# Gated linear attention and a two-expert router in one kernel: router weights through SyncE, routing regrouped into thirteen steps, first gathers of x issued later in their stage

## The chip, the cores and the metric

The kernel runs on one core of a Trainium2 chip. The metric is the device time of one execution in microseconds. Three runs of the kernel before took 773.51, 774.62 and 775.79 us; their median is 774.62 us. A separate execution was recorded by the hardware profiler; all timelines below are from it.

Engines are named as the profile names them: PE is TensorE (PEld its weight loads), DVE is VectorE, ACT is ScalarE, POOL is GpSimd, SP is SyncE, which only issues DMAs. A name with a q (ACTq, SPq) is an engine's queue, here the issue of DMAs.

## What is computed

The first block is a recurrence over 768 positions for 4 batches and 8 heads of 48 dimensions. Its output, as 3072 rows x of 384 numbers, feeds a router that picks two of eight experts for each row; each expert is a two-layer network.

```python
for t in range(S):
    state = alpha[:, :, t, :, None] * state + einsum('bhd,bhe->bhde', k[:, :, t], v[:, :, t])
    y[:, :, t] = einsum('bhd,bhde->bhe', q[:, :, t], state)
x = y.transpose(0, 2, 1, 3).reshape(3072, 384)
noisy = x @ w_gate + log1p(exp(x @ w_noise)) * noise        # (3072, 8)
top2  = the two largest of each row; top2_w = their softmax
for e in range(8):
    for k in range(2):
        mask = top2[:, k] == e
        out[mask] += top2_w[mask, k, None] * (relu(x[mask] @ w1[e]) @ w2[e])
```

All data are float32; w1 is 8 x 384 x 1024, w2 is 8 x 1024 x 384.

## The kernel before

**Chunks.** The 3072 rows are cut into 24 chunks of 128 positions, six to a batch. For a chunk n, `load` and `load_v` bring a (alphas), k, q and v of all heads by SyncE (L159, L163); an input has three buffers. `alphas` transposes a on TensorE (L304) into a PSUM tile tp, ScalarE copies it to a_all (L312), and VectorE forms the running products P_all by a scan (L315), a reciprocal (L320) and the products over by a scan backwards (L321). `keys` transposes k (L304), copies it (ScalarE, L330), checks the alphas (L333), and GpSimd multiplies by over to give k_P (L334). `queries` transposes q (L304); VectorE multiplies it by P_all out of PSUM to q_P (L343), and GpSimd copies the last column of P_all (P_end, L344). tp has two buffers for all these transposes; a_all, P_all and over have one each. `scores` multiplies k_P and q_P (sc, L354), `masked` copies them under a causal mask (MT, VectorE, L359), `turn_k` transposes k_P back (L366, copy L368), `state` updates the 48x48 states S (products L381, VectorE L383, GpSimd L384; left out at a batch's last chunk), `output` forms y (L231 and L235, copied by L238), and `turn_y` multiplies y by to_rows (L250), which turns it to rows and at once gives the router's logits; ScalarE takes lgs and y_sb out (L253, L256), and `put_y` stores the rows to x_rows in DRAM (SyncE, L260).

**to_rows.** It holds, for each pair of heads, an identity part and the columns of w_gate and w_noise. `load_router` clears it (GpSimd, L172), copies the identity parts (L176) and loads the weights straight into place in eight DMAs issued by ScalarE (L182), then the noise in one more (L184), which `turn_noise` transposes two chunks later (L190).

**Routing.** Six chunks make a unit u (four in all). `routing(u)` is a generator: each `yield` ends a step. Steps: `sum_logits` (L595), `noisy_logits` (two activations, L600, L601), `best` twice (L610 to L616), `gates` (L632), `choose_rest` (L638 to L653: normalise, mark the picked experts, sum to chosen), `count_past` (L658 to L661: how many rows of the earlier chunks went to each expert), `enter` (TensorE products rank of chosen and of past, L667 and L668, then places, L669 to L676), and `plan_tiles`, which works out which expert each tile of 128 rows belongs to (L727 to L799), with `order_slots` (L701 to L718) within it for the first plan. With the plans of unit 1, the 17 tiles that must be full by then become known; the plan of unit 3 gives the rest. `ROUTE` lists (chunk, place) for each step; the last unit has its own list. Twelve indirect DMAs of GpSimd per unit (L134) write the rows' entries into a table in DRAM, three to a chunk (`put_some`).

**Experts.** For a tile i, `load_tab` reads 128 entries of the table (tab; SyncE for early tiles, L820, after all table writes that may fill it), `load_w1` the first-layer weights (SyncE, L828, 1.5 MB), `gather_x` works out row numbers (VectorE, L837 to L843) and gathers x rows by an indirect DMA of GpSimd (L845), `turn_x` transposes them (L854, copy L856), `layer1` is 48 products (L865), `layer2` 16 (L877). The results are added to what an earlier tile left in `out` (L884, L898, L902). Parts of w2 are loaded by SyncE beside this (L205), ordered by a slot that `order_slots` gives each expert.

**Order of the work.** The kernel writes out the order of issue itself, and each engine runs its own instructions in that order. The loop goes over n, the chunk whose state and output are formed. In stage n the pieces are, by place: 0 loads, `put_y(n - 2)` and `state(n)`; 1 `alphas(n + 2)`; 2 `keys(n + 2)`; 3 `scores(n + 1)`; 4 `queries(n + 2)` and `masked(n + 1)`; 5 parts of w2; 6 `turn_k(n + 1)`; 7 `output(n)`; 8 `turn_y(n - 1)`. After each piece comes `route(n, place)`, which runs the steps of routing that the list has there. `put_some(3)` ends a stage. From n = 23 two tiles of experts share a stage. Stage 20 ends with the tab loads of tiles 0 to 3; stage 21 has `load_w1(0)` and the first two `gather_x` ahead of place 1; stage 22 ends with `load_w1(1)` and `turn_x(0)`.

Of the kernel before, what the change touches and what calls it, by code (L numbers as in the profile page):

```python
# [18 lines left out]
def kernel(  # L19
# [150 lines left out]

    def load_router(on):
        nc.gpsimd.memset(to_rows, 0.0)  # L172
        for i in range(2):
            for odd in range(2):
                pairs = to_rows.rearrange("p (j o) c -> p j o c", o=2)[:, :, odd]
                nc.gpsimd.tensor_copy(out=pairs[:, :, ds(2 * E * odd + D * i, D)],  # L176
                                      in_=ident[:, None, ds(DP * i, D)].to_broadcast([C, NP // 2, D]))
        for w, src in enumerate((moe_w_gate, moe_w_noise)):
            for i, part in enumerate(src.rearrange("(j o i d) e -> i o d j e", o=2, i=2, d=D)):
                for odd in range(2):  # L180
                    pairs = to_rows.rearrange("p (j o) c -> p j o c", o=2)[:, :, odd]
                    nc.scalar.dma_start(out=pairs[ds(DP * i, D), :, ds((1 - odd) * 2 * D + E * w, E)], in_=part[odd])  # L182
        by_chunk = on["two"].tile([C, KO * F], F32, tag="w1", name="by_chunk")[0:NT, 0:C * E]
        nc.scalar.dma_start(out=by_chunk, in_=moe_noise.rearrange("(n p) e -> n (p e)", p=C))  # L184
        return by_chunk.rearrange("n (p e) -> n e p", e=E)
# [10 lines left out]
    slot_of = const.tile([C, EV], F32, name="slot_of")  # L196
    expert_in = const.tile([C, E], I32, name="expert_in")
# [65 lines left out]
    def fast_gla(on):  # L263
# [138 lines left out]
        ROUTE = ((2, 0), (2, 2), (2, 5), (3, 5), (4, 2), (4, 5), (5, 5), (6, 3), (6, 5), (7, 1), (7, 5), (8, 1))  # L402
        ROUTE_LAST = ((2, 0), (2, 2), (2, 4), (2, 5), (3, 1), (3, 2), (3, 4), (4, 1), (4, 4), (4, 6), (5, 1), (5, 3))
# [168 lines left out]
    def routing(u, on, planned=True):  # L572
        lg = sum_logits(u, on)
        yield
        noisy = noisy_logits(lg, on)
        yield
        top, at = best(u, on, lg, noisy, 0)
        yield
        best(u, on, lg, noisy, 1, top, at)
        entry, at_f = choose(on, top, at)  # L580
        yield
        gates(entry)
        yield
        picked, chosen = choose_rest(u, on, entry, at_f)
        yield
        past = count_past(u, on, chosen)
        yield
        enter(u, on, entry, at_f, picked, chosen, past)
        if planned:
            yield  # L590
            yield from plan_tiles(u, on)
# [42 lines left out]
    def choose_rest(u, on, entry, at_f):  # L634
        rp = on["two"]
        w = entry[:, :, :, 1]
        den = rp.tile([C, UC, 1], F32, name="den")
        nc.vector.tensor_add(den, w[:, :, 0:1], w[:, :, 1:2])  # L638
        nc.vector.tensor_scalar(out=den, in0=den, scalar1=1e-9, scalar2=None, op0=ALU.add)
        nc.vector.reciprocal(out=den, in_=den)  # L640
        nc.vector.tensor_mul(w, w, den.to_broadcast([C, UC, 2]))
        nc.gpsimd.tensor_copy(out=entry[:, :, :, 0], in_=token_f[:, ds(u * UC, UC), None].to_broadcast([C, UC, 2]))
        for k in range(2):
            nc.gpsimd.tensor_copy(out=entry[:, :, k, 2], in_=at_f[:, 1 - k, :])


        picked = rp.tile([C, 2, UC, E], F32, name="picked")
        nc.vector.tensor_tensor(picked.rearrange("p k c e -> p (k c) e"),
                                expert_ids[:, None, :].to_broadcast([C, 2 * UC, E]),
                                at_f.rearrange("p k c -> p (k c)")[:, :, None].to_broadcast([C, 2 * UC, E]),  # L650
                                op=ALU.is_equal)
        chosen = rp.tile([C, UC, E], F32, name="chosen")
        nc.vector.tensor_add(chosen, picked[:, 0], picked[:, 1])  # L653
        return picked, chosen

    def count_past(u, on, chosen):
        past = on["two"].tile([C, UC, E], F32, name="past")
        nc.vector.tensor_copy(out=past[:, 0], in_=seen[u % 2])  # L658
        for c in range(1, UC):
            nc.vector.tensor_add(past[:, c], past[:, c - 1], chosen[:, c - 1])  # L660
        nc.vector.tensor_add(seen[(u + 1) % 2], past[:, UC - 1], chosen[:, UC - 1])  # L661
        return past
# [36 lines left out]
    def order_slots(tiles, rp):  # L699
# [4 lines left out]
        nc.vector.memset(slot_of, 0.0)  # L704
# [7 lines left out]
        nc.vector.tensor_add(slot_of[:, 0:E], slot_of[:, 0:E], other)  # L712
        at = rp.tile([C, E, E], F32, name="at_slot")
# [6 lines left out]
    def plan_tiles(u, on):  # L720
# [38 lines left out]
        def of_expert(dst, at, shape):  # L759
# [3 lines left out]
            nc.vector.tensor_scalar(out=dst, in0=dst, scalar1=0.0, scalar2=None, op0=ALU.max)  # L763
            nc.vector.tensor_tensor(dst, dst, wide(ready), op=ALU.min)
            nc.vector.tensor_tensor(dst, dst, wide(old), op=ALU.add)
# [6 lines left out]
        nc.vector.tensor_scalar(out=start, in0=start, scalar1=0.0, scalar2=None, op0=ALU.max)  # L772
        nc.vector.tensor_tensor(start, start, ready, op=ALU.min)
        nc.vector.tensor_tensor(so_far[now % 2], start, old, op=ALU.add)
        yield
        if u is not None and not lo:
            order_slots(so_far[now % 2], rp)
# [8 lines left out]
        row = rp.tile([C, K_MAX, EV], F32, name="row")[:, 0:K]  # L786
        nc.vector.scalar_tensor_tensor(row, em, float(C), region[:, None, :].to_broadcast(shape), op0=ALU.mult,
                                       op1=ALU.add)
        nc.vector.tensor_mul(row, row, behind)
        slots = rp.tile([C, K_MAX, EV], F32, name="slots")[:, 0:K]  # L790
        nc.vector.tensor_tensor(slots, behind, slot_of[:, None, :].to_broadcast(shape), op=ALU.mult)
        slot = rp.tile([C, K_MAX], F32, name="slot")[:, 0:K]
        nc.vector.reduce_sum(out=slot, in_=slots, axis=mybir.AxisListType.X)
        nc.vector.tensor_copy(out=plan[:, lo:hi, 2], in_=slot)
        first = rp.tile([C, K_MAX], F32, name="first")[:, 0:K]
        nc.vector.reduce_sum(out=first, in_=row, axis=mybir.AxisListType.X)
        nc.vector.tensor_scalar(out=plan[:, lo:hi, 1], in0=first, scalar1=float(TROWS - C), scalar2=None, op0=ALU.min)
        nc.vector.tensor_scalar(out=plan[:, lo:hi, 0], in0=of, scalar1=float(E - 1), scalar2=None, op0=ALU.min)
        nc.vector.tensor_scalar(out=em, in0=em, scalar1=float(C), scalar2=None, op0=ALU.mult)  # L799

# [188 lines left out]
    with ExitStack() as es:  # L989
# [36 lines left out]
        with tc.manual_schedule():  # L1026
# [15 lines left out]
            held.append(load_router(on))  # L1042
            for n, tiles in enumerate(beside):
# [7 lines left out]
                if n > NT:  # L1051
                    chunk.insert(5, lambda: put_some(3))
                if n == 1:
                    last.append(lambda: clear_table(on["two"]))
# [9 lines left out]
                if n == TILES_AT - 2:  # L1064
                    chunk.insert(1, lambda: (load_w1(0), [gather_x(i, unit_of[i] + 1) for i in some[:2]]))
# [54 lines left out]
```

## Time and profile before

| | |
|---|---|
| median of three runs | 774.62 us |
| profiled execution | 777.64 us |
| its span | 775.9 us |
| mean granted TensorE clock | 0.976 |
| TensorE busy | 738.4 us |
| VectorE busy | 245.4 us |
| ScalarE busy | 184.8 us |
| GpSimd busy | 278.7 us |
| first expert product (L865) starts | 203.72 us |
| last TensorE product (L877) starts | 762.62 us |

In a timeline row the columns are: start, duration, engine, line, operation, output tile, input tiles and shape; in brackets is the engine's idle time before the row and what ended it. In a list of waits: the waiting instruction, what it waited for, and the sum, number and longest in microseconds. The granted clock is the share of full speed that TensorE was given. The profile gives instructions' times on the engines; the time of a wait is put to the event that came last.

### The profile page before, as it was taken

To read this page: it belongs to the slowest core of one execution; us is meant where nothing else is said; L and a number is where in the kernel's file an instruction comes from. 1 tells how busy PE (TensorE), PEld (TensorE's weight loads), DVE (VectorE), ACT (ScalarE), POOL (GpSimd) and SP (SyncE) were. 2 spreads that over 40 slices of the span, in tenths; PEclk is the share of its full clock that TensorE was granted. 3 is DMA by queue.
4 is the path that set the end of the run, shared out by engine and by line. 5 is a ranking of instruction groups with operands and counts; after the bars stand their busy time and mean duration, and the time that the engine had idled before them with its cause. 6 is when DMAs were issued, how large, how long until landed. Compare 5 with 4: busy or idle time off the path is not lost.

```text
span 775.9 us, 14815 instructions
## 1 busy us (share of the span) xinstructions
PE 738.4 (95%) x5479; PEld 599.2 (77%) x5479; DVE 245.4 (32%) x820; ACT 184.8 (24%) x385; POOL 278.7 (36%) x373
## 2 busy tenths in 40 slices
PE   5699998988999999999999999999999999999995
PEld 4588887866887777886788778887788877887784
DVE  6467876996311222331110111101111111101111
ACT  2255645443112221111111111111111111111110
POOL 4222355454123363454332233332333323332222
PEclk9799999997799999999999999999999999999999
DMA  9699887773989965456555554455555565556641
GB/s 153 79 168 155 143 138 126 130 139 86 366 281 309 304 220 203 152 190 204 193 172 184 205 193 157 161 189 206 191 163 180 208 210 186 175 197 210 223 129 33
DMA packets 149092, 141.81 MB, mean 183 GB/s; under 512 B 111785, under 2 KB 123671, under 8 KB 149012
## 3 DMA queue, kind: packets, MB, share of 16 engines
q1 hardware_dynamic: 135712, 116.45, 53.9%
q0 software_dynamic: 12224, 23.78, 10.3%
q8 instruction: 47, 0.77, 0.4%
q10 hardware_dynamic: 1076, 0.53, 0.3%
q14 instruction: 33, 0.27, 0.1%
HBM read 131.95 MB, written 15.25 MB: 190 GB/s over the span
## 4 chain that ended last, share of the span: by engine, by line
PE 68%; issue 13%; DVE 7%; POOL 5%; DMA 4%; ACTq 1%; ACT 1%; another core or an unknown queue 0%; POOLq 0%; SPq 0%; DVEq 0%
PE h_ps L865 26%; PE o_ps L877 25%; PE tp L304 3%; PE y L235 3%; PE y L231 3%; PE h_ps L250 2%; PE sc L354 2%; DMA x_in<-x_rows,where 2%; POOL table L134 2%; PE x_ps L854 2%; DMA prev<-out_dram,where 2%; POOL out_dram L902 1%; DVE over L321 1%; DVE P_all L315 1%; PE tp L366 1%
## 5 line engine op out<-in xcount | busy, mean ns | idle before, releaser
L865 PEld LDWEIGHTS h_ps<-xt,w 128*128 128x128 f32 x2448 | 281.0, 192 | 14.0 <-issue 1.1
L865 PE MATMUL h_ps<-xt,w 128*128 128x128 f32 x2448 | 282.2, 275 | 1.6 <-issue 0.9
L877 PE MATMUL o_ps<-w,h 128*128 x816 | 272.2, 487 | 0.3 <-issue 0.2
L877 PEld LDWEIGHTS o_ps<-w,h 128*128 128x128 f32 x816 | 151.0, 190 | 95.6 <-issue 0.9
L856 DVE COPY xt<-x_ps 128x384 f32<-128x384 f32 x51 | 28.4, 557 | 388.7 <-PE x_ps L854 297.4
L884 POOL DMA_INDIRECT prev<-out_dram,where x51 | 52.5, 1030 | 243.8 <-DMA out_dram<-prev,where 231.5
L867 ACT ACTIVATE h<-h_ps 128x512 f32<-128x512 f32 x102 | 60.9, 597 | 221.6 <-PE h_ps L865 194.0
L893 ACT ACTIVATE o<-o_ps,tab 128x384 f32<-128x384 f32 x49 | 28.4, 580 | 239.4 <-PE o_ps L877 229.9
L902 POOL DMA_INDIRECT out_dram<-prev,where x51 | 52.6, 1031 | 91.4 <-DVE tab L839 68.9
L304 PE MATMUL tp<-ident,w 128*128 128x128 f32 x288 | 46.0, 297 | 18.1 <-ACT a_all L312 7.8
L845 POOL DMA_INDIRECT x_in<-x_rows,where x51 | 52.9, 1038 | 28.4 <-issue 13.3
L334 POOL TENSOR_TENSOR k_P<-k_P,over 128x512 f32<-128x512 f32 x24 | 28.4, 1183 | 76.5 <-DVE over L321 68.2
L134 POOL DMA_INDIRECT table<-entry,place_u x48 | 48.2, 1005 | 14.1 <-issue 13.1
L304 PEld LDWEIGHTS tp<-ident,w 128*128 128x128 f32 x288 | 33.1, 149 | 24.1 <-ACT a_all L312 8.5
L898 DVE SCALAR_TENSOR_TENSOR prev<-prev,tab,o 128x384 f32<-128x384 f32 x49 | 30.0, 611 | 51.2 <-DMA prev<-out_dram,where 45.2
L354 PE MATMUL sc<-q_P,k_P 48*128 48x128 f32 x384 | 31.4, 299 | 6.7 <-POOL k_P L334 6.4
L315 DVE TENSOR_TENSOR_SCAN P_all<-a_all,least 128x516 f32<-128x516 f32 x24 | 29.9, 1246 | 23.0 <-ACT a_all L312 15.9
L354 PEld LDWEIGHTS sc<-q_P,k_P 48*128 48x128 f32 x384 | 26.1, 199 | 11.5 <-POOL k_P L334 7.2
L359 DVE COPY_PREDICATED MT<-upto,sc 128x512 f32<-128x512 uint32 x48 | 32.0, 721 | 3.4 <-PE sc L354 3.4
L231 PE MATMUL y<-q_P,S 48*64 48x128 f32 x384 | 30.0, 302 | 0.0
L321 DVE TENSOR_TENSOR_SCAN over<-a_all,P_all 128x515 f32<-128x515 f32 x24 | 29.5, 1230 | 0.8
L235 PE MATMUL y<-MT,vt 128*48 128x128 f32 x384 | 29.4, 302 | 0.0
(155 smaller groups left out, 485.7 us busy)
## 6 DMA issues: line engine op xcount, KB each, us to landing
w<-in_moe_w_dram SPq DMA_DIRECT2D x51, 1536.0 KB
w<-in_moe_w_dram SPq DMA_DIRECT2D x32, 384.0 KB
w<-in_alpha_dram SPq DMA_DIRECT2D x24, 192.0 KB
w<-in_k_dram SPq DMA_DIRECT2D x24, 192.0 KB
w<-in_q_dram SPq DMA_DIRECT2D x24, 192.0 KB
vt<-in_v_dram SPq DMA_DIRECT2D x24, 192.0 KB
x_rows<-y_sb SPq DMA_DIRECT2D x24, 192.0 KB
x_in<-x_rows,where POOLq DMA_INDIRECT x51
```

The lines of the kernel that those rows point to most:

```text
L134: put = nc.gpsimd.indirect_dma_start(out=table, out_offset=bass.IndirectOffsetOnAxis(ap=place, axis=0), in_=entry, in_offset=None, bounds_ ...
L231: nc.tensor.matmul(y[ds(DP * i, DP), j, :], S_old[ds(DP * i, D), j, :], q[ds(DP * i, D), j, :], start=j == 0, stop=False, skip_group_check ...
L235: nc.tensor.matmul(y[ds(DP * i, D), j, :], v[:, 2 * j + i, :], MT[:, i, j, :], start=False, stop=True, skip_group_check=True)
L304: nc.tensor.transpose(tp[:, j, :], src[:, 2 * j:2 * j + 2, :], ident)
L315: nc.vector.tensor_tensor_scan(P_all[:, 0:NP * CB], a_all[:, 0:NP * CB], least.rearrange("p j t -> p (j t)"), 0.0, op0=ALU.mult, op1=ALU.max)
L354: nc.tensor.matmul(c["sc"][i][:, j, :], c["k"][r, j, :], c["q"][r, j, :], start=True, stop=True)
L845: nc.gpsimd.indirect_dma_start(out=x_in[i % NB], out_offset=None, in_=x_rows[0:units * UT, :], in_offset=bass.IndirectOffsetOnAxis(ap=wher ...
L865: nc.tensor.matmul(h_ps[:, fo, :], w1[:, a, ds((part * FO // 2 + fo) * C, C)], xt[:, a, :], start=a == 0, stop=a == KO - 1)
L867: nc.scalar.activation(os_[i]["h"][part], h_ps, AF.Relu)
L877: take_w2(i, nc.tensor.matmul(o["ps"], o["h"][part][:, f, :], w2[:, ds(o["e"], 1), fo, :].rearrange("p o d -> p (o d)"), start=fo == 0, st ...
L884: get = nc.gpsimd.indirect_dma_start(out=prev[i % 2].bitcast(U32), out_offset=None, in_=out.bitcast(U32), in_offset=bass.IndirectOffsetOnA ...
L902: put = nc.gpsimd.indirect_dma_start(out=out, out_offset=bass.IndirectOffsetOnAxis(ap=where[:, 0:1], axis=0), in_=rows, in_offset=None, bo ...
```

## The change

It has four parts.

1. The clearing of to_rows and its identity parts come at the start of the program. The router weights are loaded in four DMAs of SyncE into a tile of their own, w_r, in stage 0 ahead of place 1, and the noise in a fifth; in stage 1, behind place 5, GpSimd copies w_r into to_rows in two operations (`place_router`).
2. Routing has thirteen steps instead of twelve. `choose_rest` and `count_past` become one step; `order_slots` and the last part of `plan_tiles` are cut in two; `enter` and what follows come earlier. Some operations are merged (a maximum and a minimum in one; slots and first rows in one reduction and one store), and an addition of zeros is left out.
3. The addition to chosen and all of `count_past` run on GpSimd.
4. In stage 21 the first two `gather_x` move from ahead of place 1 to behind the last piece.

```diff
+    nc.gpsimd.memset(to_rows, 0.0)
+    for i in range(2):
+        for odd in range(2):
+            nc.gpsimd.tensor_copy(
+                out=to_rows.rearrange("p (j o) c -> p j o c", o=2)[:, :, odd, ds(2 * E * odd + D * i, D)],
+                in_=ident[:, None, ds(DP * i, D)].to_broadcast([C, NP // 2, D]))
+
     def load_router(on):
-        nc.gpsimd.memset(to_rows, 0.0)
...
+        w_r = on["one"].tile([C, NP, 2, E], F32, name="w_r")
+        nc.gpsimd.memset(w_r, 0.0)
         for w, src in enumerate((moe_w_gate, moe_w_noise)):
...
-                    nc.scalar.dma_start(out=pairs[ds(DP * i, D), :, ds((1 - odd) * 2 * D + E * w, E)], in_=part[odd])
+            for i, part in enumerate(src.rearrange("(j i d) e -> i d j e", i=2, d=D)):
+                nc.sync.dma_start(out=w_r[ds(DP * i, D), :, w, :], in_=part)
+        return w_r, load_noise(on)
+
+    def place_router(w_r):
+        for odd in range(2):
+            nc.gpsimd.tensor_copy(
+                out=to_rows.rearrange("p (j o) c -> p j o c", o=2)[:, :, odd, ds((1 - odd) * 2 * D, 2 * E)],
+                in_=w_r.rearrange("p (j o) w e -> p j o (w e)", o=2)[:, :, odd])
+
+    def load_noise(on):
...
-        nc.scalar.dma_start(out=by_chunk, in_=moe_noise.rearrange("(n p) e -> n (p e)", p=C))
+        nc.sync.dma_start(out=by_chunk, in_=moe_noise.rearrange("(n p) e -> n (p e)", p=C))
...
-        ROUTE = ((2, 0), (2, 2), (2, 5), (3, 5), (4, 2), (4, 5), (5, 5), (6, 3), (6, 5), (7, 1), (7, 5), (8, 1))
-        ROUTE_LAST = ((2, 0), (2, 2), (2, 4), (2, 5), (3, 1), (3, 2), (3, 4), (4, 1), (4, 4), (4, 6), (5, 1), (5, 3))
+        ROUTE = ((2, 0), (2, 2), (2, 5), (3, 5), (4, 2), (4, 5), (5, 3), (5, 5), (6, 5), (7, 1), (7, 5), (8, 1), (9, 1))
+        ROUTE_LAST = ((2, 0), (2, 2), (2, 4), (2, 5), (3, 1), (3, 4), (4, 1), (4, 4), (4, 6), (5, 0), (5, 1), (5, 3))
...
         picked, chosen = choose_rest(u, on, entry, at_f)
-        yield
         past = count_past(u, on, chosen)
...
-        nc.vector.tensor_add(chosen, picked[:, 0], picked[:, 1])
+        nc.gpsimd.tensor_add(chosen, picked[:, 0], picked[:, 1])
...
-        nc.vector.tensor_copy(out=past[:, 0], in_=seen[u % 2])
+        nc.gpsimd.tensor_copy(out=past[:, 0], in_=seen[u % 2])
         for c in range(1, UC):
-            nc.vector.tensor_add(past[:, c], past[:, c - 1], chosen[:, c - 1])
-        nc.vector.tensor_add(seen[(u + 1) % 2], past[:, UC - 1], chosen[:, UC - 1])
+            nc.gpsimd.tensor_add(past[:, c], past[:, c - 1], chosen[:, c - 1])
+        nc.gpsimd.tensor_add(seen[(u + 1) % 2], past[:, UC - 1], chosen[:, UC - 1])
...
         nc.vector.tensor_add(slot_of[:, 0:E], slot_of[:, 0:E], other)
+        yield
         at = rp.tile([C, E, E], F32, name="at_slot")
...
-            nc.vector.tensor_scalar(out=dst, in0=dst, scalar1=0.0, scalar2=None, op0=ALU.max)
-            nc.vector.tensor_tensor(dst, dst, wide(ready), op=ALU.min)
-            nc.vector.tensor_tensor(dst, dst, wide(old), op=ALU.add)
+            nc.vector.scalar_tensor_tensor(dst, dst, 0.0, wide(ready), op0=ALU.max, op1=ALU.min)
+            if lo:
+                nc.vector.tensor_tensor(dst, dst, wide(old), op=ALU.add)
...
+        yield
+        both = rp.tile([C, 2, K_MAX, EV], F32, name="both")[:, :, 0:K]
+        nc.vector.tensor_tensor(both[:, 0], em, region[:, None, :].to_broadcast(shape), op=ALU.add)
+        nc.vector.tensor_mul(both[:, 0], both[:, 0], behind)
+        nc.vector.tensor_tensor(both[:, 1], behind, slot_of[:, None, :].to_broadcast(shape), op=ALU.mult)
+        first = rp.tile([C, 2, K_MAX], F32, name="first")[:, :, 0:K]
+        nc.vector.reduce_sum(out=first, in_=both, axis=mybir.AxisListType.X)
+        nc.vector.tensor_scalar(out=plan[:, lo:hi, 1:3].rearrange("p k w -> p w k"), in0=first, scalar1=float(TROWS - C),
+                                scalar2=None, op0=ALU.min)
...
-            held.append(load_router(on))
...
+                if n == 0:
+                    chunk.insert(1, lambda: held.extend(load_router(on)))
                 if n == 1:
+                    chunk.insert(6, lambda: place_router(held.pop(0)))
                     last.append(lambda: clear_table(on["two"]))
...
                 if n == TILES_AT - 2:
-                    chunk.insert(1, lambda: (load_w1(0), [gather_x(i, unit_of[i] + 1) for i in some[:2]]))
+                    chunk.insert(1, lambda: load_w1(0))
+                    chunk.append(lambda: [gather_x(i, unit_of[i] + 1) for i in some[:2]])
```

## The prediction, made before the changed kernel ran

> **What bounds the kernel now.** I read the engines' busy time first: TensorE is busy for 738 of 775.9 us, so a gain can come from two places only, its 37 us of waiting and the time in which it works at a lowered clock. The next view is the list of TensorE's waits over the whole run.
>
> ```profile
> PE tp L304 <- ACT a_all L312: 7.8, 3, 6.1
> PE sc L354 <- POOL k_P L334: 6.4, 2, 4.0
> PE tp L304 <- issue: 3.5, 3, 1.5
> PE x_ps L854 <- DMA x_in<-x_rows,where: 2.4, 3, 1.3
> PE tp L304 <- DVE q_P L343: 2.3, 2, 1.5
> ```
>
> Columns: microseconds in all, times, longest. Two single waits stand out, 6.1 us and 4.0 us. Then I asked for the stages they lie in (columns: stretch, length, busy time and count per engine, granted clock, DMA share, GB/s).
>
> ```profile
> 20.00:25.00 5.00, 0.09 (x2) 0.00 (x0) 0.00 (x0) 0.00 (x0) 0.84 (x3) 0.66 0.97 102
> 25.00:30.00 5.00, 3.76 (x24) 3.14 (x24) 3.66 (x5) 2.26 (x5) 0.87 (x1) 0.50 0.10 21
> 170.00:180.00 10.00, 8.35 (x73) 6.67 (x73) 9.62 (x31) 3.05 (x9) 6.02 (x7) 0.76 0.69 175
> 190.00:205.00 15.00, 10.26 (x82) 8.94 (x79) 9.41 (x32) 1.60 (x6) 4.79 (x9) 0.66 0.94 325
> 240.00:300.00 60.00, 57.65 (x357) 46.06 (x356) 13.91 (x81) 13.14 (x24) 23.90 (x27) 1.00 0.84 283
> ```
>
> Each wait is followed by a stretch at clock 0.50: sixteen L231 products take 1.97 us there instead of 1.09. So a wait costs itself and then half of the work of the next 3.4 to 10 us. From 205 to 700 us TensorE runs at clock 1.00 and nearly without a gap; nothing is to be had there. The timeline names the causes.
>
> ```profile
> 19.45 2.28 ACTq L182 DMA_DIRECT2D to_rows<-in_moe_w_gate_dram  x4
> 24.84 0.64 ACTq L184 DMA_DIRECT2D by_chunk<-in_moe_noise_dram  x1
> 25.60 0.58 ACT L312 COPY a_all<-tp 128x512 f32<-128x512 f32 x1 [9.40 <-DMA by_chunk<-in_moe_noise_dram]
> ...
> 158.84 1.18 POOL L334 TENSOR_TENSOR k_P<-k_P,over 128x512 f32<-128x512 f32 x1 [2.86 <-DVE over L321]
> 158.94 1.17 DVE L763 TENSOR_SCALAR given<-given 128x153 f32<-128x153 f32 x1
> 162.40 0.65 PE L304 MATMUL tp<-ident,w 128*128 128x128 f32 x4 [0.78 <-DVE q_P L343]
> 173.21 0.66 PE L304 MATMUL tp<-ident,w 128*128 128x128 f32 x4 [1.52 <-issue]
> ...
> 186.88 3.24 SPq L820 DMA_DIRECT2D tab<-table  x4
> 188.58 0.23 DVE L837 SCALAR_TENSOR_TENSOR other<-expert_idv,tab,given 128x8 f32<-128x8 f32 x1 [3.43 <-DMA tab<-table]
> 190.27 1.23 DVE L315 TENSOR_TENSOR_SCAN P_all<-a_all,least 128x516 f32<-128x516 f32 x1
> 194.37 2.63 PE L354 MATMUL sc<-q_P,k_P 48*128 48x128 f32 x16 [4.04 <-POOL k_P L334]
> ```
>
> Nine DMAs issued by ScalarE stand ahead of its copy of chunk 2's alphas; planning on VectorE stands ahead of q_P, which holds the PSUM bank that TensorE wants; and the first gather's wait for tab stands ahead of the last chunk's scan.
>
> **1. Router weights to SyncE.** Without the nine issues, the copy of a_all starts when its last reader ends (over of chunk 1, 17.55). VectorE is free at 18.39 and GpSimd has read the old P_all at 19.0, so the scan starts near 19.1 instead of 26.27. TensorE's transposes of q follow its scores at 20.1 instead of 26.24: 6.1 us. The work behind them, up to the transposes at 32.36, runs at clock 1: 3.9 us by the rows of the next chunk instead of 6.1, so 2.2 more. Together 8.3.
> What now comes late: SyncE takes five issues behind the load of chunk 4 (issued to 20.17). At the 0.57 to 0.65 us that ScalarE's took, they end near 23.5, and only then come v and inputs of chunks 3 and 5, which wait for the first output anyway (32.0 before, about 23.5 now). The initial loads fill the DMA engines until about 23; the weights land near 25.5. GpSimd places them in two copies (0.22 us each, from its 128x96 copies) behind k_P and P_end of chunk 3, so near 30.1, while TensorE asks for to_rows near 29.3: it waits 0.8. The memset and four copies (0.47 and 0.89) move to the start, between the first memsets of the input tiles; the first transposes at 4.27 wait for the alphas' DMA, and those memsets end under it: nothing, at most 0.3. Net gain 7.5; bounds 5.5 and 8.3.
>
> **2. Routing in thirteen steps.** Unit 1's planning puts 3.1 us of VectorE (158.61 to 161.75) ahead of q_P in chunk 18's stage and 3.6 us (168.96 to 172.55) in the next. The new steps put there nine small operations (about 0.17 each, 1.5 us), then five (1.3 to 1.9), then six in a third stage (1.7). Where no planning runs, q_P ends 2.2 us before TensorE wants its bank (112.27, and the transposes of k near 114.5), so 1.5 to 1.9 fits. The stalls of 0.78 and 1.52 go, and with them the half-clock stretches behind them (about 3.4 and 6.8 us, half of it lost: 5.1). That is 7.4. But part stays: groups of three table writes (GpSimd L134, 1.3 us apart) coincide with late hand-overs from TensorE, and the stages behind them wait 0.65, 1.30, 0.51 and 1.12 us. Unit 1's groups come one chunk earlier, as many as before, three in full stages: 3 x 0.8 = 2.5 against the 1.12 counted, plus one half-clock stretch of 1.7. Net gain 4.5; bounds 0 and 8.5.
>
> **3. Counting on GpSimd.** Eight dependent operations per unit (0.17 to 0.25 us each on VectorE) go to GpSimd, and one step is merged: TensorE's rank product now comes less than one stage after the choice. In the stage at 93 us, VectorE ends the choice at 94.0 and TensorE would reach the product at 96.1. No row shows so small an addition on GpSimd. Its smallest copies take 0.16 to 0.19, its 192- and 512-element products 0.51 and 1.18, a line that ends near 0.12; with a dependency 0.15 to 0.3. I take 0.24 (the small copy plus its semaphore): the chain ends at 95.6, no wait. But the scan P_all starts at 95.4 and lasts 1.23.
> Two rules speak against the change here. GpSimd's product L384 took 1.45 at 116.92, beside the scan P_all (116.85, 1.23), and 0.51 elsewhere; behind this row stands the Trainium skill, "SBUF — State Buffer", section "SBUF: two separate sides": VectorE with two SBUF inputs and GpSimd hold a shared port as an exclusive lock, and the later one waits for the whole instruction. By it the last additions wait out one scan (rank 0.9 late) or two (2.9). And "GPSIMD Engine Reference", section "3. Performance versus the Vector engine", has GpSimd about half as fast at an addition: 0.4 each instead of VectorE's 0.2, the chain ends at 96.6, rank is 0.5 late even without a lock. By the copies' row it is not late. I take 0.5 for each of units 0 and 1, so 1.0 lost; bounds 0 and 2.9 each before any clock loss.
>
> **4. First gathers behind the keys' product.** From chunk 21's state product (182.80) to the first expert product (203.72) it took 20.9 us. Unit 1's table writes end a chunk earlier, so the tab loads no longer hold SyncE (idle to 186.88), and the scan isn't queued behind them. At full clock and without waits: 6.85 for the stage, then 0.6, 1.1, 1.0, 1.0, 1.1 for the next one's products, 0.5 for rank, 1.0 to the first expert product: 13.2. New waits: rank for GpSimd's count, about 0.8 (choice ends 7.6 into the stage, count 9.4, product wanted 8.6); x_in, whose gather is queued behind that count: issued near 9.6, 1.1 on GpSimd, landed 2.5 later as the first one's packets show (193.1), so 13.2 against TensorE's 13.0; and part of a half-clock stretch, 1.0. About 15.5, a gain of 5; bounds 2 and 8. The weights w1 took 7 us from issue; issued near 4.5 they are there by 11.5. In the expert stage unit 2's last group of table writes leaves the queue ahead of one gather that TensorE waited 0.97 for (292.94): 0.9 gained, bounds 0 and 1.2.
>
> Sum: 7.5 + 4.5 - 1.0 + 5.0 + 0.9 = 16.9. The profiled execution took 777.64 (span 775.9): it becomes 760.7. The median of the runs, 774.62, lies 3.0 below; the same step gives **757.7 us**.
>
> **Rivals.**
> - *Routing keeps its waits* (the late hand-overs beside the table writes, not VectorE's queue, set them; for it: ScalarE's copy at 116.18 waited 2.06 with VectorE unloaded; against it: two waits end at q_P itself). Part 2 gives 0: 762.2. Chance 0.22.
> - *The hand-over turns into a wait for x_in or w1*, since gather and count share GpSimd and w1 shares the DMA engines. Part 4 gives 1 us: 761.7. Chance 0.13.
> - *SyncE becomes the first stage's queue*: the nine issues are only moved, and loads of chunk 5 come late. Part 1 gives 3: 762.2. Against it: those loads are needed 14 us later. Chance 0.05.
> - *All these waits go and the clock stays up*: 8.3 + 8.5 + 0 + 8.2 + 1.2 = 26.2: 748.4, with 749 to 754 on the way there. Chance 0.13.
> - *Slower: rank waits for GpSimd.* If both scans lock GpSimd out, each of units 0, 1 and 2 costs 2.9 and a half-clock stretch of 10.2 us (5.1 lost, as after 192): 3 x 8.0 = 24 against the 17.9 of the rest: 780.7. It decides from 6.7 us per unit (a third of the 17.9 and of the 2.3 that a measurement can tell). Chance 0.06, of which 0.02 for a strength that ends within 0.3%.
>
> **Numbers.** My forecast, 754 to 761, has 0.41. The range 750 to 766 leaves out the rival that loses and most of the full gain. Within 0.3% (2.3 us, about what this measurement can tell from no change) 0.02; slower 0.04; faster 0.94.
>
> **What would show it.** Right: no idle TensorE from 20 to 26 us and clock 1.00 there; a rest of under 1 us before the first L250 product (now released by GpSimd); no wait released by q_P between 155 and 180; sc of the last chunk without its 4.04; the first expert product near 188. Wrong: waits at the rank products released by GpSimd additions, additions or scans of double length beside each other, half-clock slices still at 160 to 200 us, or a long wait of x_ps for x_in.

## The result, and the profile after

| | median (range), runs | ratio to before, 95% interval | profiled execution (span, mean clock) |
|---|---|---|---|
| before, same chip | 774.80 us (773.51 to 775.79), 4 | | 777.64 us (775.9, 0.976) |
| changed | 764.46 us (761.62 to 765.79), 4 | 0.9863, 0.9831 to 0.9894 | 764.23 us (762.5, 0.989) |

The changed kernel is 10.3 us faster. The forecast was 757.7 us, a gain of 16.9, most likely between 754 and 761; the wider range of 750 to 766 holds the result, near its end. TensorE is busy for 732.9 us of the span (738.4 before). These are waits of the changed kernel's TensorE (the waiting instruction, what it waited for; sum, number, longest in us). Lines below the edits have moved: x_ps is now L860, tp L315, sc L365, the rank products L677 and L678, the first layer L871.

```profile
PE tp L315 <- DMA w<-in_alpha_dram: 4.2, 1, 4.2
PE x_ps L860 <- DMA x_in<-x_rows,where: 3.8, 2, 2.8
PE sc L365 <- POOL k_P L345: 3.3, 1, 3.3
...
PE h_ps L678 <- POOL past L670: 1.5, 3, 1.1
```

The waits of 6.1 us (a_all) and 4.0 us (sc of the last chunk) are gone; the 4.2 and the 3.3 here belong to the first chunk (4.3 and 2.3 before). New is x_ps, which waits 2.8 for the first gathered rows. The view by stretches (length; busy time and number on PE, PEld, DVE, ACT, POOL; granted clock; DMA share; GB/s):

```profile
20.00:25.00 5.00, 5.00 (x77) 4.49 (x78) 4.93 (x7) 2.30 (x5) 1.77 (x4) 1.00 0.97 101
25.00:30.00 5.00, 4.67 (x61) 3.79 (x59) 4.11 (x7) 2.55 (x6) 1.82 (x4) 1.00 1.06 167
160.00:170.00 10.00, 8.75 (x102) 7.19 (x104) 9.62 (x28) 4.23 (x11) 6.75 (x8) 1.00 0.77 195
179.00:182.40 3.40, 2.29 (x28) 1.75 (x27) 2.25 (x14) 0.00 (x0) 1.95 (x9) 1.00 0.98 366
182.40:185.80 3.40, 3.40 (x24) 2.89 (x20) 0.90 (x3) 0.58 (x1) 2.91 (x6) 0.50 1.06 393
185.80:189.20 3.40, 0.56 (x4) 0.31 (x3) 0.00 (x0) 0.63 (x3) 2.63 (x3) 1.00 1.04 406
189.20:192.60 3.40, 2.75 (x13) 2.65 (x13) 1.06 (x7) 0.00 (x0) 1.72 (x3) 0.51 1.12 354
192.60:196.00 3.40, 3.40 (x18) 3.40 (x17) 0.00 (x0) 0.52 (x1) 0.65 (x1) 0.50 0.75 185
```

20 to 30 us now runs at clock 1.00 and nearly without a rest, as forecast. The stretch of unit 1's planning runs at full clock here too, but not always: in six of the twelve profiles of this document that have part 2, half clock begins between 164 and 169 us. In the hand-over to the experts (from the state product of stage 21 to the first expert product) it is the other way round: the clock falls to 0.50 after a window in which TensorE was busy for 2.29 of 3.40 us, and again after one in which it waited for x_in. The timeline of those places:

```profile
20.49 1.58 SPq L183 DMA_DIRECT2D w_r<-in_moe_w_gate_dram  x2
...
30.21 1.15 PE L261 MATMUL h_ps<-to_rows,yT 128*128 128x112 f32 x8 [0.54 <-POOL to_rows L188]
...
177.55 1.72 PE L365 MATMUL sc<-q_P,k_P 48*128 48x128 f32 x16
...
178.65 1.29 SPq L216 DMA_DIRECT2D w<-in_moe_w_dram  x2
178.93 0.28 POOL L663 TENSOR_TENSOR chosen<-picked 128x48 f32<-128x48 f32 x1 [0.91 <-DVE picked L658]
...
179.43 1.31 POOL L670 TENSOR_TENSOR past<-past,chosen 128x8 f32<-128x8 f32 x5
...
180.80 0.42 PE L678 MATMUL h_ps<-past,ones 128*128 128x48 f32 x2 [1.11 <-POOL past L670]
...
182.00 1.10 POOL L851 DMA_INDIRECT x_in<-x_rows,where  x1 [0.98 <-DVE place_u L686]
...
188.76 0.55 PE L860 MATMUL x_ps<-ident,x_in 128*128 128x128 f32 x3 [2.84 <-DMA x_in<-x_rows,where]
...
189.95 8.52 PE L871 MATMUL h_ps<-xt,w 128*128 128x128 f32 x48 [0.65 <-DVE xt L862]
```

sc no longer waits for k_P. The gather is issued at 182.00, its rows have landed 4.9 us after the issue's end, and the first tile's first layer then takes 8.52 us; the same 48 products took 5.60 before (203.72 to 209.32). Aligned by the same products of TensorE, the changed execution leads the one before by 7.3 us at the first to_rows product, by 13.0 at the state product of stage 21, by 13.8 at the first expert product, and by only 10.9 at the second tile's x_ps. So the routing stages brought 5.7 more, the hand-over 0.8, and the first tile gave back 2.9. Another 2.5 came from there to the end, 13.4 in all between these two executions.

### The profile page after: what moved, and what is told of

It reads as the page before. It is cut to its first block, busy times and chain, and to the rows that moved or that the text cites. A ratio compares the mean times of both kernels' runs of the same rounds, so it can differ in the third digit from the quotient of the medians.

```text
span 762.5 us, 14806 instructions
## 1 busy us (share of the span) xinstructions
PE 732.9 (96%) x5479; PEld 595.0 (78%) x5479; DVE 240.9 (32%) x778; ACT 184.9 (24%) x385; POOL 289.8 (38%) x409
## 3 DMA queue, kind: packets, MB, share of 16 engines
q0 software_dynamic: 12224, 23.78, 10.3%
## 4 chain that ended last, share of the span: by engine, by line
PE 69%; issue 11%; DVE 9%; POOL 4%; DMA 4%; ACT 1%; another core or an unknown queue 0%; POOLq 0%; DVEq 0%; ACTq 0%
PE h_ps L871 28%; PE o_ps L883 26%; PE tp L315 3%; DMA x_in<-x_rows,where 2%; PE h_ps L261 2%; PE y L246 2%; PE x_ps L860 2%; PE y L242 2%; PE sc L365 2%; DMA prev<-out_dram,where 2%; DVE over L332 2%; DVE P_all L326 1%; POOL out_dram L908 1%; DVE MT L370 1%; POOL table L134 1%
## 5 line engine op out<-in xcount | busy, mean ns | idle before, releaser
L871 PEld LDWEIGHTS h_ps<-xt,w 128*128 128x128 f32 x2448 | 284.0, 194 | 14.7 <-DVE again L428 1.6
L871 PE MATMUL h_ps<-xt,w 128*128 128x128 f32 x2448 | 285.0, 277 | 2.1 <-DVE again L428 1.4
L134 POOL DMA_INDIRECT table<-entry,place_u x48 | 49.9, 1039 | 14.0 <-issue 12.8
L315 PE MATMUL tp<-ident,w 128*128 128x128 f32 x288 | 44.5, 291 | 9.0 <-DMA w<-in_alpha_dram 4.2
L315 PEld LDWEIGHTS tp<-ident,w 128*128 128x128 f32 x288 | 32.3, 146 | 14.7 <-POOL w L281 4.7
L365 PE MATMUL sc<-q_P,k_P 48*128 48x128 f32 x384 | 30.8, 292 | 3.6 <-POOL k_P L345 3.3
L365 PEld LDWEIGHTS sc<-q_P,k_P 48*128 48x128 f32 x384 | 25.6, 193 | 8.3 <-issue 4.1
L860 PE MATMUL x_ps<-ident,x_in 128*128 128x128 f32 x153 | 25.2, 274 | 4.0 <-DMA x_in<-x_rows,where 3.8
L261 PE MATMUL h_ps<-to_rows,yT 128*128 128x112 f32 x192 | 28.5, 293 | 0.5 <-POOL to_rows L188 0.5
```

The lines of the kernel that those rows point to most:

```text
L134: put = nc.gpsimd.indirect_dma_start(out=table, out_offset=bass.IndirectOffsetOnAxis(ap=place, axis=0), in_=entry, in_offset=None, bounds_ ...
L261: nc.tensor.matmul(bank[:, at:at + W], yT[:, j, :], to_rows[:, j, :], start=j == 0, stop=j % 2 == 1, skip_group_check=True)
L315: nc.tensor.transpose(tp[:, j, :], src[:, 2 * j:2 * j + 2, :], ident)
L365: nc.tensor.matmul(c["sc"][i][:, j, :], c["k"][r, j, :], c["q"][r, j, :], start=True, stop=True)
L860: nc.tensor.transpose(x_ps[:, a, :], x_in[i % NB][:, ds(a * C, C)], ident)
L871: nc.tensor.matmul(h_ps[:, fo, :], w1[:, a, ds((part * FO // 2 + fo) * C, C)], xt[:, a, :], start=a == 0, stop=a == KO - 1)
```

## The experiments

Three theories were tried. (A) The first gathers come late because they now stand on GpSimd behind the last unit's choice and count. (B) They come late because their rows stand in the DMA engines behind expert weights. Against both: the gain of the hand-over had nothing to do with the place of the gathers. The first four runs of the table ran on one chip, the next four on a second, the last four on a third, each time beside the kernel before. Chips differ (its median was 774.80 in the first comparison; 773.92, 775.22 and 770.92 in the three batches), so differences are read within a batch and ratios across. The expectations call the stage with the gathers 22, by the chunk whose keys' product is formed there; it is n = 21, and "22 and 23" of one of them are n = 21 and 22.

| run | what it has | median us | less than before | ratio, 95% interval |
|---|---|---|---|---|
| after_again | all four parts | 766.46 | 7.5 | 0.9894, 0.9858 to 0.9931 |
| count_on_vector | without part 3 | 762.29 | 11.6 | 0.9831, 0.9797 to 0.9864 |
| gathers_first | without part 4 | 762.81 | 11.1 | 0.9854, 0.9820 to 0.9888 |
| gathers_middle | all, gathers ahead of the count | 763.83 | 10.1 | 0.9856, 0.9821 to 0.9890 |
| router_alone | part 1 | 768.70 | 6.5 | 0.9914, 0.9897 to 0.9931 |
| parts_1_and_2 | parts 1 and 2 | 760.72 | 14.5 | 0.9803, 0.9778 to 0.9828 |
| w2_later | all, parts of w2 put off | 766.01 | 9.2 | 0.9881, 0.9861 to 0.9901 |
| token_by_iota | all, no copy of integers | 766.25 | 9.0 | 0.9883, 0.9860 to 0.9906 |
| routing_alone | part 2 | 762.67 | 8.3 | 0.9886, 0.9864 to 0.9909 |
| parts_1_and_2_again | parts 1 and 2 | 756.12 | 14.8 | 0.9811, 0.9786 to 0.9836 |
| parts_1_and_2_iota | parts 1 and 2, no copy of integers | 757.22 | 13.7 | 0.9813, 0.9787 to 0.9839 |
| gathers_late_quiet | all, no weights beside the gathers | 762.57 | 8.4 | 0.9893, 0.9869 to 0.9917 |

**after_again.** No edit.

> The changed kernel once more, as the anchor for the runs beside it. Theory and rivals alike: 762 to 766, some 10 below the kernel before. In the hand-over (first state product of stage 21 to the first expert product) it should again take 19 to 21 us, and the first x_ps product should again wait about 2.8 for x_in.

Time 766.46, hand-over 19.97 us, x_ps waited 4.38 there. The first tile ran at half clock again. So the new wait is no accident of one execution.

**count_on_vector.**

```diff
-        nc.gpsimd.tensor_add(chosen, picked[:, 0], picked[:, 1])
+        nc.vector.tensor_add(chosen, picked[:, 0], picked[:, 1])
```

and the same for all of `count_past`.

> The changed kernel with the choice and count of a unit (chosen, past, seen) back on VectorE; all else as changed. Theory A (in the hand-over the two gathers of x stand on GpSimd behind the count of the last unit, which took 1.31 there, and x_in comes 2.8 late for that): GpSimd reaches the gathers some 1.5 earlier, x_in lands 1.0 to 1.5 earlier, the rank product loses its 1.1 of waiting, and the hand-over shortens by about 1 to 2.5; units 0 and 1 lose 0.2 each; the time is 1.5 to 3 below the changed kernel, near 762. Theory B (x_in's rows stand in the DMA engines behind w2's and w1's parts, so an earlier issue doesn't land earlier): x_ps goes on waiting for x_in about as long as the count becomes earlier, that is 3 to 4, and the time is within 1 of the changed kernel. Theory C (VectorE's own seven operations of the count lengthen its routing steps by what they did before): 1 to 2 above the changed kernel.

4.2 below after_again, more than A's 3 at most. Counted from stage 21's state product, the gather was issued at 10.5 (11.7 in after_again, 12.2 in the first profile of the changed kernel) and x_ps ran at 17.0 (18.4 and 18.9); the rank product waited 0.54 instead of 1.11, and the hand-over took 18.5. So A's chain is there, with A's size. But x_ps still waited 3.94, as B said, since TensorE was there earlier too, and the first layer still ran mostly at half clock (7.79 us). Where the rest of the 4.2 comes from is not shown by one trace.

**gathers_first** and **gathers_middle.** The two gathers in the old place, and between `masked` and the choice.

```diff
-                    chunk.insert(1, lambda: load_w1(0))
-                    chunk.append(lambda: [gather_x(i, unit_of[i] + 1) for i in some[:2]])
+                    chunk.insert(1, lambda: (load_w1(0), [gather_x(i, unit_of[i] + 1) for i in some[:2]]))
```

This is gathers_first; gathers_middle leaves `load_w1(0)` where it is and inserts the gathers behind `masked`.

> The changed kernel with the first two gathers of x back ahead of stage 22's work (part 4 undone), w1 in the same place. Prediction's theory (the gathers on SyncE's and GpSimd's queues there hold place 1's work, and with it the hand-over): the keys' product of stage 22 waits 2 to 4 longer than in the changed kernel, x_in no longer waits; sum: 1 slower to 2 slower, near 766. Theory A (the new place makes x_in late): x_in lands well ahead of its product, the wait of 2.8 goes, the wait at the keys' product comes back at about 2, and the time is within 1 of the changed kernel or up to 2 below it. Theory B (DMA traffic): the gathers issued before the burst of w2's parts land within 2.5 us as in the kernel before.

> The changed kernel with the first two gathers of x neither ahead of stage 22 nor at its end, but behind its queries and masked keys and ahead of the step that chooses and counts. Theory A (place on GpSimd is the cause): gathers issued near 178 to 179 instead of 182, x_in there before 186, the x_ps wait of 2.8 goes; the count moves some 2 later behind the gathers and the rank product waits 1 to 2 more; in sum 1 to 4 below the changed kernel. Theory B (the DMA engines are the cause): the gathers' packets stand behind w1(0)'s and w2's parts, which fill 177 to 186, x_in still lands near 187 to 188.6, and the time is within 1 of the changed kernel.

With the gathers in their old place the time is 3.7 below after_again, beyond what A gave it (2 at most) and against the prediction. The second kernel, gathers_middle, lies 2.6 below, inside A's bounds. First gathers_first, then gathers_middle:

```profile
176.75 1.10 POOL L851 DMA_INDIRECT x_in<-x_rows,where  x1 [0.67 <-DVE tab L847]
...
180.88 2.10 PE L365 MATMUL sc<-q_P,k_P 48*128 48x128 f32 x16 [1.31 <-POOL k_P L345]
...
189.65 0.49 PE L860 MATMUL x_ps<-ident,x_in 128*128 128x128 f32 x3
...
190.79 5.62 PE L871 MATMUL h_ps<-xt,w 128*128 128x128 f32 x48 [0.65 <-DVE xt L862]
```

```profile
180.70 1.10 POOL L851 DMA_INDIRECT x_in<-x_rows,where  x1 [1.14 <-DVE tab L845]
...
183.86 0.66 PE L677 MATMUL h_ps<-chosen,before 128*128 128x48 f32 x2 [2.67 <-POOL chosen L663]
```

In the old place sc waits 1.31 for k_P, not the 4.04 of the kernel before, x_ps waits for nothing, and the first layer runs at full clock in 5.62 us. In the middle place the gathers hold up the count, and TensorE waits 2.67 for chosen instead: the wait is exchanged, not removed. Its hand-over is the longest of all, 22.5 us, but here too the first layer takes 5.62.

**router_alone, parts_1_and_2, routing_alone.** Parts 1 and 2 alone and together. The first and last are the kernel before with those hunks of the diff; parts_1_and_2 is the changed kernel with both edits above.

> The kernel before with part 1 alone (router weights staged by SyncE into w_r, placed by GpSimd, cleared to_rows at the start, noise behind them on SyncE); routing, count and gathers as before. Prediction's step: 7.5 from the stage where the first router product waited, kept to the end, so about 767. Rival (what the start gains is taken back later, because the routing then runs into the same waits as before): the first router product is 7.3 earlier, but the gain at the state product of stage 21 is under 5, and the time is 769 to 772.

> The changed kernel with both the count back on VectorE and the two gathers back ahead of stage 22's work: what is left are the router's weights and the routing in thirteen steps. If parts 3 and 4 together cost time, as the two runs that undid one of them suggest (4.2 and 3.7 below the changed kernel beside them), this is the fastest so far, 759 to 762. If the two undo the same wait (x_in behind GpSimd's work), it is no better than either, 762 to 763. If count and gathers on GpSimd are a gain as predicted, it is slower than the changed kernel, above 766.

> The kernel before with part 2 alone (fewer VectorE operations, routing in thirteen steps with other places); router weights, count and gathers as before. By the difference of the two earlier runs (router_alone 768.7, parts_1_and_2 760.7, each against 775.2 of the kernel before) the routing is worth 8.0: 767 if the parts add up. Prediction's sum: 4.5, that is 770.5. Rival (it pays only once the router's weights no longer hold up the early stages): under 3, above 772.

Part 1 gives 6.5 (and 6.6 between routing_alone and parts_1_and_2_again). In its profile 8.2 stands at the first to_rows product and 8.6 at the state product of stage 21, so it is kept, and the rival in its expectation falls. Part 2 alone gives 8.3, and the pair 14.5: they add up. The pair is faster than the changed kernel, so parts 3 and 4 together cost about 0.7%, some 5.5 us: the four runs that have both in their planned places (changed, after_again, token_by_iota, w2_later) have ratios of 0.9863 to 0.9894, the three that have neither 0.9803 to 0.9813. The wait of sc, in routing_alone and then in router_alone, shows whose gain it was:

```profile
181.31 1.87 PE L355 MATMUL sc<-q_P,k_P 48*128 48x128 f32 x16 [1.31 <-POOL k_P L335]
```

```profile
PE sc L364 <- POOL k_P L344: 5.8, 2, 3.5
```

With part 2 alone, gathers in the old place, the wait is 1.31; with part 1 alone it is 3.45 (the longest of two). VectorE's wait for tab ahead of that stage's scan, 3.43 in the kernel before and 3.25 in router_alone, is in none of the four profiles with part 2 and the gathers in the old place (routing_alone, gathers_first, parts_1_and_2 and its repeat). So part 2, with its earlier table writes, took away most of sc's wait; the move of the gathers was needed for the last 1.1 to 1.3 at most.

**w2_later** and **gathers_late_quiet.**

```diff
-        w2_beside = {TILES_AT - n: parts for n, parts in ((4, 1), (3, 3), (2, 2), (1, 2))}
+        w2_beside = {TILES_AT - n: parts for n, parts in ((4, 1), (3, 3))}
```

gathers_late_quiet has this and, besides:

```diff
-                    chunk.append(lambda: (load_w1(1), turn_x(0)))
+                    chunk.append(lambda: turn_x(0))
+                if n == TILES_AT:
+                    chunk.insert(1, lambda: load_w1(1))
```

> The changed kernel with no parts of w2 loaded in stages 22 and 23 (they come later, between the first tiles' work); gathers at the end of stage 22 as changed. Theory B (the first gather's packets start 3.4 after the end of its issue because w2's 1536-byte packets fill the DMA engines from 181 to 186): they start within 1.5 of the issue's end, x_in lands 2 to 4 earlier, the wait of 2.8 to 4.4 at the first x_ps product shrinks to under 1.5, the first expert product starts 2 to 3 earlier after the state product of stage 21, 17 to 18 instead of 20. If the first tiles then wait for w2, part of that is given back. Theory A (only the place on GpSimd): packets go on starting 3 to 4 after the issue, time within 1 of the changed kernel.

> The changed kernel with the gathers at the end of the stage as changed, but neither w2's parts nor the second tile's w1 issued in the two stages ahead (w2 later, w1(1) behind the next put of y), so that from some 182 on no weights are on the way. In the run that only put off w2, SyncE ran ahead to w1(1) and its 4096-byte packets filled the DMA engines in the place of w2's. Theory B (the gather's rows stand behind weights in the DMA engines): packets start within 1.5 of the end of the first gather's issue (3.4 in the changed kernel, 0.8 in the kernel before), x_in lands 2 earlier and the wait at the first x_ps product falls from 2.8 to about 1. Theory A (the late place alone, behind the count): packets start 3 or more after the issue, the wait stays at 2.5 or more. In either case the first tiles wait for w2 as in the run before it, some 1.5, so the time is 762 to 766.

w2_later did not tell the theories apart: SyncE ran ahead and issued w1(1) at 179.42, whose packets filled the DMA engines in place of w2's. The second kernel did. The table is from the record of DMA packets, counted from the end of the first gather's issue. The bytes are those that SyncE's queue, which carries the weights, started between one microsecond before that end and the first row:

| run | SyncE's bytes meanwhile | first row starts | all rows landed |
|---|---|---|---|
| before | 0.0 MB | +0.7 us | +2.6 us |
| gathers_late_quiet | 0.1 MB | +0.7 us | +1.7 us |
| gathers_first | 0.5 MB | +1.5 us | +3.6 us |
| w2_later | 1.4 MB | +2.4 us | +3.4 us |
| gathers_middle | 1.6 MB | +3.3 us | +5.1 us |
| changed | 1.7 MB | +3.4 us | +4.9 us |

The bytes grow with the delay itself; what sets the runs apart is their rate, 370 to 410 GB/s in the last three, 200 in gathers_first and under 50 in the first two. The lines are of gathers_late_quiet:

```profile
177.06 1.10 POOL L851 DMA_INDIRECT x_in<-x_rows,where  x1 [0.98 <-DMA w<-in_moe_w_dram]
...
180.45 0.49 PE L860 MATMUL x_ps<-ident,x_in 128*128 128x128 f32 x3
...
181.59 5.62 PE L871 MATMUL h_ps<-xt,w 128*128 128x128 f32 x48 [0.65 <-DVE xt L862]
...
194.82 5.37 PE L871 MATMUL h_ps<-xt,w 128*128 128x128 f32 x46 [2.11 <-DMA w<-in_moe_w_dram]
```

The gathers stand in the late place, behind the count, and yet x_ps doesn't wait, since hardly any weights are on the way: B holds for the landing. The hand-over takes 18.25 and the first layer 5.62, but the weights put off are missed later (2.11 here), and in sum nothing is gained: 0.9893. (The profiled execution, 758.74, was the fastest of six.)

**token_by_iota** and **parts_1_and_2_iota.** The changed kernel's first stage was 0.9 us late: VectorE's copy of token numbers took 3.88 us beside GpSimd's clearings (2.60 before), and the scan behind it 2.18 instead of 1.23. More clearings alone don't explain it: in router_alone, which has the same ones but for one of 0.10 us (slot_of, from part 2), the copy took 0.16.

```diff
-    nc.vector.tensor_copy(out=token_f, in_=token)
+    nc.gpsimd.iota(token_f, pattern=[[C, NT]], base=0, channel_multiplier=1, allow_small_or_imprecise_dtypes=True)
```

> The changed kernel with token_f written by GpSimd's iota as float, with no VectorE copy of the integers at the start. Theory (that copy, 3.88 instead of 2.60 in the kernel before, is held up by GpSimd's longer series of clearings and holds up the scan behind it, so stage 0 is 0.9 late): the first state product is about 0.9 earlier than in the changed kernel; but the first router product waits for to_rows anyway, so from there on at most 0.5 stays. Rival (the scan itself is slower beside GpSimd's clearings): the first state product stays within 0.3 of the changed kernel. Time 0 to 0.5 below the changed kernel.

> Parts 1 and 2, and token_f written by GpSimd's iota as float in place of VectorE's copy. In the changed kernel that edit brought the first state product 0.8 forward and the first router product 0.4. Theory: the 0.4 stays to the end, so 0.3 to 0.6 below the run beside it, about 760. Rival: below what can be told apart, within 1 either way.

In token_by_iota the scan is back at 1.23, the first state product 0.8 earlier and the first to_rows product 0.4 earlier than in the changed kernel. In the time nothing of it can be told: 766.25 beside 766.01 of w2_later, and 757.22 beside 756.12. In the profile of parts_1_and_2_iota a gather in the middle of the expert stage came 6.0 us late; that alone hides such a gain.

> Parts 1 and 2 without 3 and 4, as before, the anchor for the run with the float iota: 759 to 762, some 14 below the kernel before. Its x_ps products should again not wait for x_in, and no half clock should fall into the first tile's first layer.

Time 756.12, on the faster chip 14.8 below the kernel before; no half clock in the first tile's first layer. x_ps waited 2.4 in two places, at later tiles: there the expectation missed.

## Why the prediction was right, and where not

- **Part 1, 7.5: right.** It is 7.3 in the profile, carried to the end, and 6.5 and 6.6 by the runs. Three of its numbers were off and nearly cancelled. The stages from 20 us on gained 8.8 (from 0.9 behind at the first state product to 7.9 ahead at the next) where 8.3 stood. To_rows made TensorE wait 0.54 instead of 0.8. The start cost 0.9 where "nothing, at most 0.3" stood; with part 1 alone it did cost 0.3, and there the copy of token numbers took 0.16, not 3.88.
- **Part 2, 4.5: right for the routing stages, but the term left out what follows them.** The runs give 8.0 (parts_1_and_2 less router_alone) and 8.3, near its upper bound of 8.5. Between stages 10 and 21 the profile of parts_1_and_2 gains 3.9 us on that of the kernel before, near the 4.5. The eight profiles with part 2 from the first comparison and the first two batches gain 2.9 to 5.7 there, router_alone 0.4. Its hand-over is another 2.1 shorter, with sc's wait down from 4.04 to 1.13. From the first expert product to the end it gains 2.2 more, whose cause isn't worked out. The prediction named the cause of the 2.1, the tab loads behind the table writes, but booked it under part 4.

  The last chip shows something else: all four of its profiles gain 12.2 to 12.4 between those stages. The late hand-overs beside the table writes are missing there. In the ten other profiles, the one of the kernel before among them, ScalarE's copy of the alphas starts 1.0 to 2.6 us after its transposes ended, in five or six stages between 100 and 175 us (chunk 16: 2.2 both before and in the changed kernel, where TensorE then waits 1.31). In the last chip's four it is never more than 0.1 late there. The kernel before wasn't profiled on that chip, where its median is 3 to 4 us lower, so these 12 are not all part 2's. The rival "routing keeps its waits" is out with its forecast of 0; but the late hand-overs that it named did stay in all eight of those other profiles with part 2.
- **Part 3, -1.0: right in sign, too small.** The additions start 0.28 apart (0.24 was assumed; 0.19 on VectorE in count_on_vector), so the 0.4 each of the prediction's second rule didn't come, and no long wait arises from their number. The last addition of unit 0 met the scan P_all and ended with it: 1.0 us instead of 0.20, in line with the exclusive lock that the prediction cites. The five took 2.12 us there, and 1.31 in the last unit, where no scan ran. It cost TensorE 0.18 and 0.19 in units 0 and 1, under the 0.5 taken; in the last unit the rank product waited 1.11 where 0.8 was taken. The loss in the runs is larger, 4.2 when part 3 is undone alone, and its cause is shown only in part. The additions of unit 0 and the scan:

```profile
87.25 2.12 POOL L670 TENSOR_TENSOR past<-past,chosen 128x8 f32<-128x8 f32 x5
...
88.12 1.25 DVE L326 TENSOR_TENSOR_SCAN P_all<-a_all,least 128x516 f32<-128x516 f32 x1 [0.88 <-ACT a_all L323]
```

- **Part 4, +5.0: wrong.** With part 4 the hand-over took 20.1 us, not 15.5; without it (gathers_first) 20.2, and then the first tile's first layer was 2.9 us shorter. Two terms failed. "Issued near 9.6" came to 12.2, since the choice ended 1.4 later than taken, the count took 2.2 instead of 1.8, and GpSimd stood still for 0.98 between the count and the gather, with the row numbers ready since 179.42 (0.98 too in after_again, w2_later and gathers_late_quiet). "Landed 2.5 later, as the first one's packets show" came to 4.9, since that row of before was measured with no weights on the way, and the earlier tab had brought w1 and w2 forward to this very place. So for this term the rival "the hand-over turns into a wait for x_in" held. The wait was followed by half clock in the first tile, 2.9 us, where the sum had 1.0 for part of one such stretch.
- **Unit 2's table writes, +0.9: the wait is gone.** In the changed kernel tile 8's gather isn't waited for (0.97 before). From the second tile to the end 2.5 us were gained; what else is in them isn't worked out.
- **The step from the profiled execution to the median.** The sum was made on an execution 3.0 above its median and carried over whole. The changed kernel's profiled execution, 764.23, lies at its own median: the two profiled executions differ by 13.4, the medians by 10.3. A slower than usual execution may hold waits that others don't have; how many of the 3 us these are isn't shown.

All four signs of being wrong that the prediction named are in the profile: waits of the rank products for GpSimd additions, an addition of more than double length beside a scan, half clock after 160 us, and a long wait of x_ps. That the result is in the range all the same is in part luck: part 2 gave some 3.5 more than taken, while parts 3 and 4 together took 5.5 where 4.0 of gain stood. By the measured parts the gain is 6.5 + 8.3 - 5.5 = 9.3; the four runs with all parts gave 7.5 to 10.3. How the cost splits between parts 3 and 4 stays open: undone singly they give 4.2 and 3.7, together about 5.5 (0.0071 of 775), so they overlap in part, and each of these has an interval of some 3 us.

Half clock decides what these waits cost. Within the kernel its stretches last 3.41 us or a multiple: 3.41, 6.83 or 10.24. The Trainium skill, "TensorE: Matmul & The Clock Gate", section "Part 1: The HAM clock gate", has a free-running window of 3413 ns after which the clock is halved or freed, which fits. Of when it bites, its section "HAM oscillation — how this bites in real kernels" says "The abstract rule is 'no PE-idle gaps >~3.4µs.'" By that rule alone even the wait of 2.84 us would have cost only itself. The stretches above show otherwise: a window in which TensorE still worked for two thirds, with one wait of 1.11, was followed by one at 0.50.

```profile
177.40:180.80 3.40, 2.23 (x28) 1.81 (x26) 3.30 (x7) 1.12 (x4) 2.71 (x6) 1.00 0.91 275
180.80:184.20 3.40, 3.33 (x22) 3.04 (x24) 2.49 (x14) 0.00 (x0) 0.51 (x1) 0.50 1.01 403
```

These two are of parts_1_and_2: sc's wait of 1.13 is enough there too. It isn't certain each time: in after_again a window with 0.61 of work (116.8 to 120.2) was followed by full clock. Cut into these windows, up to 740 us, the fourteen profiles of this document give a count. Of the full-clock windows, all 11 in which TensorE was busy for less than 0.43 of the time were followed by half clock, 25 of the 71 between 0.43 and 0.735, and none of the 2841 above. What decides in the middle isn't shown.

## What to carry to other kernels

Take the latency of a small gather from a row with the same traffic beside it: what is moved later may land among transfers that the same change has brought forward. Before crediting a move with the end of a wait, ask which of the change's parts makes the waited-for data earlier, and try the parts singly; here two of four gave 14.5 us and the other two took more than a third of it back. Count a wait in a nearly full engine with what the clock adds to it. And compare a profile only with one from the same chip, or with several: the same kernel, parts_1_and_2, led the one profile of the kernel before by 11.2 us at stage 21 on one chip and by 19.7 on another.

## What was not expected of the hardware

The rows of an indirect DMA of GpSimd started 0.7 us after its issue on idle DMA engines, and 3.3 to 3.4 us after it when weights went out meanwhile on SyncE's queue at some 370 to 400 GB/s. The Trainium skill, "DMA: Bandwidth & Descriptors", section "Queues, rings and completion order", has each DMA engine take turns between its queues packet by packet; by that the rows would have started after a few of the weights' packets. In the changed kernel some 2.5 MB of weights had been issued and not yet started when the gather's issue ended, and 1.4 MB of them went out before its first row. Where this delay arises no run here shows.
